# Reordering the per-unit vector work inside the matmul groups of an mLSTM and MLP kernel

## The chip, the cores and the metric

The kernel runs on one core of a Trainium2 chip. The time is that of the device in microseconds (us), the median of several runs. PE is TensorE, ACT is ScalarE, DVE is VectorE, POOL is GpSimd, and SP is SyncE, which here only issues transfers.

## The reference

Two stages follow each other. An mLSTM recurrence runs over 768 time steps for 4 batches of 8 heads with 40 features each, and a two-layer MLP is applied to its 3072 output rows of 320 features.

```
m_new  = maximum(f_gate + m, i_gate)
f_stab = exp(f_gate + m - m_new);  i_stab = exp(i_gate - m_new)
C = f_stab * C + i_stab * outer(v, k)
n = f_stab * n + i_stab * k
y = sigmoid(o_gate) * (C @ q) / maximum(abs(n . q), 1)
...
h = x @ w_in                     # 320 -> 2048
out = (h * sigmoid(h)) @ w_out   # 2048 -> 320
```

All inputs and the output are float32.

## The kernel before, in words

**Units.** The recurrence is cut into 24 units: a unit is one chunk of 64 time steps for half of the batches, 128 rows. Inside a unit the recurrence is a masked attention of the chunk with itself plus a term with the state `Cm` that earlier chunks left. Three units (384 rows) make one step of the MLP, so there are 8 steps.

**MLP.** The 2048 hidden features of a step are 16 chunks of 128. For chunk `k` the first product goes into a PSUM bank (`spot`), ACT computes a tanh (`rise`, L922), DVE the gated value `th` (L925), ACT a rounded high part `gh` (L934), DVE the remainder `gl` (L938, both of `part`), and the second product accumulates into `pout`. Both products are made from high parts and remainders, three matmuls for one, as pairs on the two halves of the array's rows. From chunk 18 on (`FIRST`) a group `k` of the last loop issues on PE the upper half of chunk `k` and the lower half of chunk `k-1`, and the second product of chunks `k-4` and `k-3`. `first_product` of group `k` lets its lower half wait for the tanh of chunk `k-2`.

**Blocks.** Into the groups of step `j` the three units of step `j+1` are woven; they are called A, B and C here. `places` gives the groups: 3, 7 and 11 in step 1, and 1, 5 and 9 from step 2 on. `at[0]` is the unit whose block stands in this group, `at[1]` the one whose block stood a group ago, and so on. A block (`block`) is, on PE between the first and second products, the scores of the next unit, the unit's own values, and the new state (`state`, L733), for which two `spot` banks are taken; the second is the one that the `th` of the same group gives back. Then follow, on DVE, the division and the output gate (`norm`, `level`, `scale`) and a 32-wise transpose into the single buffer `xt` (`turn_out`, L804), and on POOL the state's decay (`carry`: multiply L783, add L792).

**Around a block.** In the later groups a unit is transposed through memory: SP writes `xt` out (`turn_away`, L810, in `at[1]`) and reads it as `px` (`turn_in`, L818, in `at[3]`; for C in `at[1]`). `xput` then puts it in front of the next step's first product: ACT rounds `px` to `xh` (L847) and DVE takes the remainder `xl` (L848), for A and B in `at[6]`, for C in `at[4]`. So A's `xput` is in the group that is `at[2]` of B, and B's in that of C.

**Preparing the next units.** `turn` loads units ahead and makes on POOL the decay exponents `am` (`shift`, L530). In `at[2]` come `misc` of the next unit (`gate`, a tanh on ACT, L544; `look`, an exponential on ACT, L551; `near`, the scaled queries `qt` on POOL, L555) and `add` of the one after (POOL, L538); in `at[3]` the exponential of `D` (`exp`, ACT, L541) and the weighted keys (`keys`, DVE, L590).

**Weights.** The weights of the first pass through the MLP are used whole; for the others each of 8 pieces of `w_in` and `w_out` is split once into a high part (ACT: L345 for `i`, L336 for `o`) and a remainder (DVE: L347, L338) by `split_in` and `split_out`. `LOWS` names the chunk in whose tanh and `gh`/`gl` these two instructions are put.

**Order.** Each engine runs its instructions in program order, written by hand: what stands behind a waiting instruction on an engine waits too.

Of the kernel before, what the change touches and what calls it, by code (L numbers as in the profile page):

```python
# [22 lines left out]
NU = NC * NP  # L23
# [3 lines left out]
UPS = 3  # L27
# [15 lines left out]
FIRST = NFC + LAG  # L43
# [3 lines left out]
def mlstm_mlp_kernel(  # L47
# [281 lines left out]
    def split_out(i):  # L329

        if not woh:
            woh[0] = pg.tile([128, NFC, DM], F32R, tag="g", name="woh")
        full, hi = wo.pop(i), woh[0][:, 2 * i : 2 * i + 2, :]
        to, tag = (pq, "wo") if i else (pw, "wt")
        wol[i] = to.tile([128, 2, DM], F32R, tag=tag, name=f"wol{i}")
        nc.scalar.copy(hi, full)  # L336
        yield
        nc.vector.tensor_tensor(out=wol[i], in0=full, in1=hi.bitcast(F32), op=ALU.subtract)  # L338

    def split_in(i):  # L340

        whole, hi = wi.pop(i), wh[:, 0:2, i * WC : (i + 1) * WC]
        to, tag = (pi, "wi") if i else (pw, "wt")
        wl[i] = to.tile([128, 2, WC], F32R, tag=tag, name=f"wl{i}")
        nc.scalar.copy(hi, whole)  # L345
        yield
        nc.vector.tensor_tensor(  # L347
            out=wl[i], in0=whole, in1=hi.bitcast(F32), op=ALU.subtract
        )
# [652 lines left out]
    units = [Unit(n) for n in range(NU)]  # L1002
    AROUND = set(range(2 * UPS, NU)) - {3 * UPS - 1}
    free, spot = [], {}
    steps = {}
# [66 lines left out]
    for _ in range(2):  # L1072
# [115 lines left out]
    SPLITS = {"i": split_in, "o": split_out}  # L1188
# [3 lines left out]
        (0, 15): ["i2"],  # L1192
        (1, 0): ["i3"],
        (1, 1): ["o0"],
        (1, 3): ["o1"],
        (1, 4): ["i4"],
        (1, 5): ["o2", "i5"],
        (1, 7): ["o3"],
        (1, 8): ["i6"],
        (1, 9): ["o4"],  # L1200
        (1, 11): ["i7"],
        (1, 12): ["o5"],
        (1, 13): ["o6"],
        (1, 14): ["o7"],
    }
    KEYS = {5: 4, 8: 5, 12: 6, 15: 7}

    def places(k):
        j, fc = divmod(k, NFC)
        if j >= NSTEP - 1:  # L1210
            return {}
        return {fc - a: units[(j + 1) * UPS + u] for u, a in enumerate(PLACES[min(j, 2)])}

    def splits(k):
        return [SPLITS[x[0]](int(x[1])) for x in LOWS.get(divmod(k, NFC), ())]

    for k in range(FIRST):
        j, fc = divmod(k, NFC)
        st, at = steps[j], places(k)
        if j == 0 and fc in KEYS:  # L1220
            units[KEYS[fc]].keys()
        st.mm1(fc)
# [26 lines left out]
    def relay(m):  # L1249

        turn = nc.scalar.nop(nofuse=True)
        tc.add_manual_dep(turn.ins, m.ins.name, WAIT, reason="row tiles")
        return turn
# [5 lines left out]
    def first_product(k, lo, hi, turn=None):  # L1259

        both = []
        if k <= LAST:
            if lo == 0:
                spot[k] = free.pop(0)
            both.append((0, k, steps[k // NFC].rows(k % NFC, 0)))
        if k > FIRST:
            both.append((1, k - 1, steps[(k - 1) // NFC].rows((k - 1) % NFC, 1)))
        n = len(both[0][2])
        for i in range(lo, min(hi, n)):
            cols = (slice(0, NT),)  # L1270
            if i > 0 and more[0] > 0:
                more[0] -= 2 * len(both)
                cols = (slice(0, NT // 2), slice(NT // 2, NT))
            for c in cols:
                for h, g, (w, x) in [(h, g, ops[i]) for h, g, ops in both]:
                    m = nc.tensor.matmul(  # L1276
                        spot[g][:, c],
                        w,
                        x[:, c],
                        start=(h == 0 and i == 0),  # L1280
                        stop=(h == 1 and i == n - 1),
                        skip_group_check=True,
                    )
                    if h == 1:
                        follow(m, turn)
                        turn = None
        return m

    def second_product(p, k, turn=None):

        st, fc = steps[k // NFC], k % NFC
        if fc == 0 and p == 0:
            st.po = [psO.tile([128, DM], F32, tag="o", name=f"pout{st.j}_{t}") for t in range(UPS)]
        for f in (fc, fc + 1):
            gh, gl = st.g[f]
            hi, lo = woh[0][:, f, :], wol[f // 2][:, f % 2, :]
            for i, (g, w) in enumerate(((gh, hi), (gh, lo), (gl, hi))):
                for h in range(2):
                    t = (p + h) % UPS
                    m = nc.tensor.matmul(  # L1300
                        st.po[t],
                        g[half(h), t * UT : (t + 1) * UT],
                        w[half(h)],
                        start=(f == 0 and i == 0 and (p, h) in ((0, 0), (0, 1), (1, 1))),
                        stop=(f == NFC - 1 and i == 2 and (p, h) in ((1, 0), (2, 0), (2, 1))),
                        skip_group_check=True,
                    )
                    follow(m, turn)
                    turn = None
        return m  # L1310

    last_turn, rises = None, {}
    for k in range(FIRST, LAST + 2):
        at = places(k)
        even = k % 2 == 0
        old = k - 4 - k % 2
        ready = FIRST - LAG <= old and k <= LAST
        if k == FIRST:
            last_turn = relay(first_product(k, 0, 8))
        elif k == FIRST + 1:  # L1320
            first_product(k, 0, 8, last_turn)
            last_turn = None
        elif even and ready:
            first_product(k, 0, 4, rises[k - 2])
            last_turn = relay(second_product(0, old, last_turn))
            first_product(k, 4, 8)
        else:
            first_product(k, 0, 8, rises[k - 2])
        new = steps[(k - 1) // NFC]
        parts = splits(k - 1)  # L1330
        if k > FIRST:
            new.rise((k - 1) % NFC, parts)
            rises[k - 1] = new.tanh
        if 0 in at:
            block(at[0].n)
        last = steps[old // NFC] if ready and old % NFC == NFC - 2 else None
        if ready:
            m = second_product(1 if even else 2, old, last_turn)
            if 0 not in at:
                for t in ((1,) if even else (0, 2)) if last else ():  # L1340
                    last.store(t)
                last_turn = relay(m)
        if k > FIRST:
            new.part((k - 1) % NFC, parts)
        if 0 in at:
            n = at[0].n
            late = n in AROUND and n % UPS == UPS - 1
            if n + 1 < NU and not late:
                units[n + 1].weigh()
            at[0].norm()  # L1350
            at[0].hold()
            if ready:
                last_turn = relay(m)
            at[0].level()
            at[0].scale()
            at[0].carry(steps=(0,))
            at[0].carry(steps=(1,))
            if at[0].n in AROUND:
                at[0].turn_out()
            if n + 1 < NU and late:  # L1360
                units[n + 1].weigh()
        if 1 in at:
            n = at[1].n
            if n in AROUND and n % UPS == UPS - 1:
                at[1].turn_away()
                if n + 2 < NU:
                    units[n + 2].load_q()
                    units[n + 2].shift()
                at[1].turn_in()
                if n + 3 < NU:  # L1370
                    units[n + 3].load()
            else:
                turn(n)
                if n in AROUND:
                    at[1].turn_away()
        if 2 in at and at[2].n + 1 < NU:
            units[at[2].n + 1].misc()
            if at[2].n + 2 < NU:
                units[at[2].n + 2].add()
        if 3 in at and at[3].n + 2 < NU:  # L1380
            units[at[3].n + 2].exp()
            units[at[3].n + 2].keys()
        if 3 in at and at[3].n in AROUND and at[3].n % UPS < UPS - 1:
            at[3].turn_in()
        for back in (4, 6):
            if back in at and at[back].n in AROUND and (at[back].n % UPS == UPS - 1) == (back == 4):
                at[back].xput(steps[k // NFC + 1])

    st = steps[NSTEP - 1]
    st.mm2(NFC - 4)  # L1390
# [82 lines left out]
```

## Time and profile before

| | |
|---|---|
| time, median of 3 runs | 456.69 us (456.0 to 457.86) |
| time of the profiled execution | 454.56 us |
| its span, first to last instruction | 452.8 us |
| PE busy | 429.4 us (95%) |
| DVE, ACT, POOL busy | 289.3, 220.9, 152.0 us |
| mean granted TensorE clock | 0.988 of full speed |

The last loop runs from about 85 us to the end. Busy time of PE is modelled at the ends of matmuls, so a row of PE that starts after a wait tells more than the share. Where ACT begins the tanh of a group the group's first product has just ended, so that the distances between these rows are the lengths of the groups.

### The profile page before, as it was taken

How to read it: one execution, taken by the hardware profiler on the slowest of the kernel's cores; microseconds unless marked ns; L12 is line 12 of the kernel's file. 1: busy time of each engine (PE TensorE's matmuls, PEld its weight loads, DVE VectorE, ACT ScalarE, POOL GpSimd, SP SyncE). 2: the span in 40 equal slices, each digit the busy share in tenths (PEclk: the TensorE clock that was granted, in tenths of full speed). 3: DMA queues.
4: the chain of work that ended last, by engine and by line, in shares of the span. 5: the costliest groups of instructions: out<-in, count | busy, mean ns of one | idle time of the engine just before them, and what ended most of it. 6: DMA issues, size and time to landing. Idle time of an engine off the chain costs nothing.

```text
span 452.8 us, 16276 instructions
## 1 busy us (share of the span) xinstructions
PE 429.4 (95%) x6864; PEld 392.7 (87%) x6864; DVE 289.3 (64%) x588; ACT 220.9 (49%) x481; POOL 152.0 (34%) x168
## 2 busy tenths in 40 slices
PE   8999999998899989999899998999989999999996
PEld 4667677898789989899889998899988999999995
DVE  5788889378786675466764665646766566544442
ACT  7694867465464443444443532435344344434331
POOL 5835234064623634045521454215632321000000
PEclk9999999999999998999999996999999999999999
DMA  8999989165410666026560375504744041101001
GB/s 250 358 364 260 291 246 232 45 157 164 126 41 15 181 184 183 8 42 184 151 189 4 116 178 129 143 4 144 178 99 145 3 104 38 36 1 45 1 2 45
DMA packets 63401, 57.60 MB, mean 127 GB/s; under 512 B 31808, under 2 KB 49936, under 8 KB 63328
## 3 DMA queue, kind: packets, MB, share of 16 engines
q1 hardware_dynamic: 63056, 56.20, 44.2%
q8 instruction: 54, 0.88, 0.8%
q10 hardware_dynamic: 208, 0.26, 0.2%
q14 instruction: 19, 0.16, 0.1%
q0 software_dynamic: 64, 0.10, 0.1%
HBM read 49.09 MB, written 7.36 MB: 125 GB/s over the span
## 4 chain that ended last, share of the span: by engine, by line
PE 43%; issue 25%; DMA 10%; DVE 8%; ACT 7%; POOL 5%; SPq 1%; POOLq 0%; ACTq 0%; DVEq 0%
PE spot L1276 16%; PE pout L1300 14%; DVE th L925 4%; PE pout L973 4%; PE ph L891 4%; ACT D L541 2%; DMA wro<-in_w_out_dram 2%; DVE xl L848 2%; DMA vb<-in_vp_dram 2%; PE p L659 2%; DMA wri<-in_w_in_dram 2%; ACT th L922 2%; DMA D<-LFd 2%; POOL D L538 2%; PE spot L733 1%
## 5 line engine op out<-in xcount | busy, mean ns | idle before, releaser
L1276 PE MATMUL spot<-xh,wh 64*128 64x384 f32 (+1 forms) x674 | 142.4, 342 | 5.5 <-ACT th L922 4.9
L1300 PE MATMUL pout<-woh,gh 64*128 64x320 f32 x648 | 121.0, 315 | 0.0
L1300 PE MATMUL pout<-wol,gh 64*128 64x320 f32 x648 | 118.8, 308 | 0.4 <-DVE wol L338 0.4
L1300 PE MATMUL pout<-woh,gl 64*128 64x320 f32 x648 | 118.8, 308 | 0.0
L1276 PE MATMUL spot<-xl,wh 64*128 64x384 f32 (+1 forms) x569 | 117.3, 334 | 0.0
L922 ACT ACTIVATE th<-spot 128x384 f32<-128x384 f32 x110 | 53.8, 489 | 116.4 <-PE spot L1276 116.2
L938 DVE TENSOR_TENSOR gl<-th,gh 128x384 fp32r<-128x384 f32 x112 | 65.9, 589 | 57.2 <-ACT gh L934 53.1
L1276 PEld LDWEIGHTS spot<-xh,wh 64*128 64x128 f32 x674 | 92.4, 186 | 10.1 <-ACT th L922 6.8
L925 DVE SCALAR_TENSOR_TENSOR th<-th,spot 128x384 f32<-128x384 f32 x110 | 60.4, 549 | 63.2 <-ACT th L922 63.1
L934 ACT CAST gh<-th 128x384 fp32r<-128x384 f32 x112 | 57.4, 513 | 77.5 <-DVE th L925 71.5
L1276 PE MATMUL spot<-xh,wl 64*128 64x384 f32 (+1 forms) x454 | 92.7, 334 | 0.0
L1300 PEld LDWEIGHTS pout<-woh,gh 64*128 64x128 f32 x648 | 81.3, 186 | 0.9
L1300 PEld LDWEIGHTS pout<-wol,gh 64*128 64x128 f32 x648 | 81.1, 187 | 0.7 <-DVE wol L338 0.7
L1300 PEld LDWEIGHTS pout<-woh,gl 64*128 64x128 f32 x648 | 80.9, 187 | 0.0
L1276 PEld LDWEIGHTS spot<-xl,wh 64*128 64x128 f32 x569 | 73.4, 187 | 0.0
L783 POOL TENSOR_TENSOR Cm<-Cm,lq 40x328 f32<-40x328 f32 x40 | 33.3, 831 | 118.7 <-PE p L659 117.2
L1276 PEld LDWEIGHTS spot<-xh,wl 64*128 64x128 f32 x454 | 60.7, 187 | 0.0
L555 POOL TENSOR_TENSOR qt<-qk,lq 104x512 f32<-104x512 f32 x22 | 29.1, 1324 | 88.8 <-ACT lq L551 59.2
L848 DVE TENSOR_TENSOR xl<-px,xh 128x384 fp32r<-128x384 f32 x17 | 30.5, 1796 | 8.1 <-ACT xh L847 8.1
L792 POOL TENSOR_TENSOR Cm<-Cm,pk 40x328 f32<-40x328 f32 x32 | 28.4, 887 | 2.4
L973 PE MATMUL pout<-wo,g 128*128 128x320 f32 x96 | 29.0, 436 | 0.0
L538 POOL TENSOR_TENSOR D<-D,am 128x512 f32<-128x512 f32 x20 | 26.1, 1304 | 6.8 <-DVE wo L302 4.5
(161 smaller groups left out, 554.8 us busy)
## 6 DMA issues: line engine op xcount, KB each, us to landing
qk<-in_qk_dram SPq DMA_DIRECT2D x24, 512.0 KB, 6.2
ko<-in_ko_dram SPq DMA_DIRECT2D x24, 320.0 KB, 5.2
wro<-in_w_out_dram SPq DMA_DIRECT2D x8, 640.0 KB, 6.0
wri<-in_w_in_dram SPq DMA_DIRECT2D x8, 512.0 KB, 5.5
D<-LFl SPq DMA_DIRECT2D x32, 128.0 KB, 3.2
lq<-LFl SPq DMA_DIRECT2D x32, 128.0 KB, 4.0
vb<-in_vp_dram SPq DMA_DIRECT2D x48, 82.0 KB, 5.0
out_dram<-ob SPq DMA_DIRECT2D x45, 80.0 KB, 2.1
```

The source lines that it names most:

```text
L538: nc.gpsimd.tensor_tensor(out=self.Dm, in0=self.Dm, in1=self.am, op=ALU.add)
L555: nc.gpsimd.tensor_tensor(out=self.qt, in0=self.q[:KS], in1=self.lq[:KS], op=ALU.mult)
L783: nc.gpsimd.tensor_tensor(out=v, in0=v, in1=self.lq[r, :, L - 1].unsqueeze(2).broadcast_to([D, H, D1]), op=ALU.mult,)
L792: nc.gpsimd.tensor_tensor(out=v, in0=v, in1=self.both[r].rearrange("p d j f -> p (d j) f"), op=ALU.add)
L848: nc.vector.tensor_tensor(out=lo, in0=px[:, a, :], in1=hi.bitcast(F32), op=ALU.subtract)
L922: self.tanh = nc.scalar.activation(th, ph, AF.Tanh, scale=0.5)
L925: nc.vector.scalar_tensor_tensor(out=th, in0=th, scalar=1.0, in1=ph, op0=ALU.add, op1=ALU.mult)
L934: nc.scalar.copy(gh, th)
L938: nc.vector.tensor_tensor(out=gl, in0=th, in1=gh.bitcast(F32), op=ALU.subtract)
L973: nc.tensor.matmul(self.po[t], g[:, ts], w, start=(fc == 0 and i == 0), stop=(last and i == len(ops) - 1), skip_group_check=(j == NSTEP - 1),)
L1276: m = nc.tensor.matmul(spot[g][:, c], w, x[:, c], start=(h == 0 and i == 0), stop=(h == 1 and i == n - 1), skip_group_check=True,)
L1300: m = nc.tensor.matmul(st.po[t], g[half(h), t * UT : (t + 1) * UT], w[half(h)], start=(f == 0 and i == 0 and (p, h) in ((0, 0), (0, 1), (1 ...
```

## The change

`gate` of the next unit goes from `at[2]` to the block's own group, behind `hold` and its wait. `carry` does multiply and add of one half before the other half. `add` goes from `at[2]` to the end of `at[1]`, the exponential of `D` from `at[3]` to `at[2]`, and `xput` stands ahead of `look` and `near` instead of behind them and `turn_in`. The weight pieces `i4` and `o1` are split in group 18 behind its first product, `i5`, `i6` and `i7` at the end of the groups with the blocks of units 6, 7 and 8, and `o2`, `o4` and `o5` one group earlier than before.

```diff
@@ LOWS
-        (1, 3): ["o1"],
-        (1, 4): ["i4"],
-        (1, 5): ["o2", "i5"],
+        (1, 4): ["o2"],
         (1, 7): ["o3"],
-        (1, 8): ["i6"],
-        (1, 9): ["o4"],
-        (1, 11): ["i7"],
-        (1, 12): ["o5"],
+        (1, 8): ["o4"],
+        (1, 11): ["o5"],
...
+    BEHIND = {2 * UPS: ["i5"], 2 * UPS + 1: ["i6"], 2 * UPS + 2: ["i7"]}
@@ the loop over groups
-        if k > FIRST:
+        if k == FIRST:
+            for x in (split_in(4), split_out(1)):
+                next(x)
+                next(x, None)
+        else:
             new.rise((k - 1) % NFC, parts)
             rises[k - 1] = new.tanh
@@ if 0 in at
                 last_turn = relay(m)
+            if n + 1 < NU:
+                units[n + 1].gate()
             at[0].level()
             at[0].scale()
-            at[0].carry(steps=(0,))
-            at[0].carry(steps=(1,))
-            if at[0].n in AROUND:
+            at[0].carry()
+            if n in AROUND:
                 at[0].turn_out()
             if n + 1 < NU and late:
                 units[n + 1].weigh()
+            for x in BEHIND.get(n, ()):
+                for _ in SPLITS[x[0]](int(x[1])):
+                    pass
@@ behind turn, in if 1 in at
-        if 2 in at and at[2].n + 1 < NU:
-            units[at[2].n + 1].misc()
-            if at[2].n + 2 < NU:
-                units[at[2].n + 2].add()
-        if 3 in at and at[3].n + 2 < NU:
-            units[at[3].n + 2].exp()
-            units[at[3].n + 2].keys()
-        if 3 in at and at[3].n in AROUND and at[3].n % UPS < UPS - 1:
-            at[3].turn_in()
+            if n + 2 < NU:
+                units[n + 2].add()
         for back in (4, 6):
             if back in at and at[back].n in AROUND and (at[back].n % UPS == UPS - 1) == (back == 4):
                 at[back].xput(steps[k // NFC + 1])
+        if 2 in at:
+            n = at[2].n
+            if n + 1 < NU:
+                units[n + 1].look()
+                units[n + 1].near()
+            if n + 2 < NU:
+                units[n + 2].exp()
+        if 3 in at:
+            n = at[3].n
+            if n + 2 < NU:
+                units[n + 2].keys()
+            if n in AROUND and n % UPS < UPS - 1:
+                at[3].turn_in()
```

## Rows read from the trace of the kernel before

**Rows 1.** Waits of PE: line, releaser, us in total, times, longest us.

```profile
PE spot L733 <- DVE th L925: 9.9, 10, 1.6
PE spot L1276 <- ACT th L922: 4.9, 6, 1.0
```

**Rows 2.** Timeline of PE, step 3: start, duration, instruction, idle before and releaser.

```profile
221.63 0.47 PE L733 MATMUL spot<-vb,kw 64*40 64x41 f32 x26 [1.54 <-DVE th L925]
...
235.52 0.44 PE L1276 MATMUL spot<-xh,wh 64*128 64x384 f32 x1 [1.01 <-ACT th L922]
```

**Rows 3.** Timeline of ACT, step 3, groups 6 to 9 and 12 to 14.

```profile
211.36 0.49 ACT L922 ACTIVATE th<-spot 128x384 f32<-128x384 f32 x1 [3.21 <-PE spot L1276]
...
213.49 0.49 ACT L922 ACTIVATE th<-spot 128x384 f32<-128x384 f32 x1
214.60 0.51 ACT L934 CAST gh<-th 128x384 fp32r<-128x384 f32 x1 [0.62 <-DVE th L925]
215.02 0.47 ACT L544 ACTIVATE ko<-ko 128x320 f32<-128x320 f32 x1
215.39 0.62 ACT L551 ACTIVATE lq<-lq 104x512 f32<-104x512 f32 x1
215.91 0.50 ACT L847 CAST xh<-px 128x384 fp32r<-128x384 f32 x1
216.68 0.49 ACT L922 ACTIVATE th<-spot 128x384 f32<-128x384 f32 x1 [0.27 <-PE spot L1276]
...
219.97 0.62 ACT L541 ACTIVATE D<-D 128x512 f32<-128x512 f32 x1
220.50 0.47 ACT L922 ACTIVATE th<-spot 128x384 f32<-128x384 f32 x1
...
231.18 0.49 ACT L922 ACTIVATE th<-spot 128x384 f32<-128x384 f32 x1 [0.27 <-PE spot L1276]
...
235.00 0.47 ACT L922 ACTIVATE th<-spot 128x384 f32<-128x384 f32 x1
...
238.18 0.49 ACT L922 ACTIVATE th<-spot 128x384 f32<-128x384 f32 x1 [1.14 <-PE spot L1276]
```

**Rows 4.** Timeline of DVE, step 3.

```profile
213.40 0.56 DVE L938 TENSOR_TENSOR gl<-th,gh 128x384 fp32r<-128x384 f32 x1 [0.58 <-ACT gh L934]
...
216.50 2.55 DVE L848 TENSOR_TENSOR xl<-px,xh 128x384 fp32r<-128x384 f32 x1 [0.79 <-ACT xh L847]
...
225.27 0.58 DVE L804 STREAM_TRANSPOSE xt<-x 128x384 f32<-128x384 f32 x1 [0.78 <-DMA xd<-xt]
...
237.13 0.55 DVE L848 TENSOR_TENSOR xl<-px,xh 128x384 fp32r<-128x384 f32 x1
```

**Rows 5.** Timeline of POOL, step 3.

```profile
211.66 1.04 POOL L530 TENSOR_TENSOR am<-mask,aT 128x512 f32<-128x512 f32 x1
216.09 1.30 POOL L555 TENSOR_TENSOR qt<-qk,lq 104x512 f32<-104x512 f32 x1 [3.38 <-DMA D<-LFl]
217.34 1.29 POOL L538 TENSOR_TENSOR D<-D,am 128x512 f32<-128x512 f32 x1
```

**Rows 6.** Timeline of ACT, step 1: a tanh, and one weight copy.

```profile
89.03 0.49 ACT L922 ACTIVATE th<-spot 128x384 f32<-128x384 f32 x1 [2.77 <-PE spot L1276]
...
100.44 0.72 ACT L336 CAST woh<-wo 128x640 fp32r<-128x640 f32 x1
```

**Rows 7.** Timeline of SP, step 3: the two reads of A and B.

```profile
212.58 0.47 SPq L818 DMA_DIRECT2D px<-xd x1
...
225.22 0.38 SPq L818 DMA_DIRECT2D px<-xd x1
```

**Rows 8.** DMA issues of the page: count, KB each, us from issue to landing.

```profile
px<-xd SPq DMA_DIRECT2D x17, 192.0 KB, 2.5
```

**Rows 9.** Stretches behind block C, steps 2 and 4; after POOL: granted clock, DMA share, GB/s.

```profile
169.00:173.05 4.05, 4.05 (x34) 4.05 (x34) 2.29 (x6) 0.00 (x0) 3.54 (x4) 0.58 0.38 85
...
278.00:283.00 5.00, 5.00 (x44) 5.00 (x44) 1.59 (x5) 0.49 (x1) 2.71 (x3) 0.62 0.45 108
```

## The prediction, on record before the change was run

> **What bounds the kernel now.** I read the waits of PE first, then the timelines of PE, ACT, DVE and POOL over one step of the last loop, then SP and the transfers, then the granted clock. PE waits for little: ten times for the `th` that gives a block its second bank and six times for a tanh, 14.8 us in all [rows 1]. The size of these waits is better read from the tanh rows of ACT, one per group. In step 3 they lie 2.13 us apart (211.36 to 213.49) and 3.19 us apart (213.49 to 216.68), which is what PE needs for an odd and an even group; but 216.68 to 220.50 is 3.82 us where 2.13 is due, so block C's tanh is 1.69 late, and 231.18 to 235.00 is again 1.69 too long [rows 3]. PE shows these as 1.54 and 1.01 [rows 2]. Nothing of it is won back: the group behind the second takes 3.18 us (235.00 to 238.18), the usual length [rows 3]. So in this loop a tanh that comes late by some time costs that time whole.
>
> Why they are late: A's `xl` on DVE begins at 216.50 and takes 2.55 us; C's, with nothing on POOL, takes 0.55 [rows 4]. During the long one POOL runs `near` (216.09, 1.30 us) and `add` (217.34 to 218.63) [rows 5]; `xl` ends at 219.05, 0.42 behind the end of `add`. So DVE's subtraction of two SBUF tiles makes hardly any headway while POOL works, and `th`, `gh`, the exponential of `D` (219.97) and the tanh (220.50) queue up behind it without a gap [rows 3].
>
> The Trainium skill, SBUF — State Buffer, section Who interferes with whom, says that a DVE instruction with two SBUF inputs contends with a GpSimd one that reads SBUF, and that the one that starts first holds the shared ports for its whole length. The 2.55 against 0.55 agrees; by the rule the moved `add` is sure to hold up whichever such subtraction of DVE arrives during it, by the rows alone that could be nothing and the sum below some 4 us lower, 435.
>
> **The change, part by part.** *`xput` first, `add` away.* `xh` comes right behind `gh`, `xl` before `near` has started, so 2.0 us of blocking go from each of A's and B's `xl`. C's lateness of 1.69 occurs in five steps (1 to 5), the one behind B's `xput` (two groups after it, 235.00) in four (2 to 5): 5 x 1.69 + 4 x 1.69 = 15.2. The other five waits for `th`, small ones before block B and one in step 1, are what is left of 9.9 after 5 x 1.54: 2.2. The two other waits for a tanh are 4.9 - 4 x 1.01 = 0.9 [rows 1, 2]. They come from the exponential of `D` or weight copies just ahead of a tanh, both of which are moved. Together 18.3 to be had.
>
> *What it puts in the way.* The exponential now stands in the `xput` group. ACT there has from `gh` at 214.60 to the tanh at 216.68. The slots by the distances of the rows: `gh` 0.42, `look` 0.52, exponential 0.53 (219.97 to 220.50), `xh` about 0.41 (its 0.50 less the overlap that `gh` shows): 1.88, to 216.48, so 0.20 in hand [rows 3]. The `gate` (0.37 of a slot) goes to the block's group, where ACT stands idle for 3.21 before the next tanh [rows 3]: nothing; without that idle time it would cost its 0.37.
>
> `add` now runs right behind `am`, from 212.70 to 213.99 [rows 5]. `gl` begins at 213.40 there [rows 4]; by the 0.42 above it ends at 214.41, not at 213.96. `th` and `gh` behind it move by 0.45, the chain ends at 216.93, and the tanh is 0.25 late. In the groups behind A, which have no `xput` on ACT, the same delay fits. So 0.25 in each of two groups in four steps: 2.0. Lower bound nothing, if DVE gets in between `am` and `add`; upper bound 0.45 each, 3.6. I take 2.0. In `add`'s old place nothing is left that waits for it: the exponential comes a group earlier and POOL has finished by then.
>
> *`carry`.* Four instructions as before; the first add now needs `hold`'s copies sooner, but the state is read eight or more groups later: nothing, at most one wait on POOL.
>
> *Weights.* `i4` and `o1`: two copies on ACT, each no longer than `o`'s 0.72 us, in group 18, where ACT stands idle for 2.77 before the tanh at 89.03 [rows 6]; the remainders fit on DVE likewise: nothing. `i5` to `i7` come behind blocks, in ACT's idle time; on DVE they stand between `xt` and the next `th`, with `am` and `add` on POOL at their side, and `o3` to `o5` share their groups with a `gl` that `add` holds up. Bounds for the groups behind B and C of step 1: 0.25 each as in other steps, 0.5, or a whole blocked row of subtractions each, 1.69 as seen, 3.4. I take 2.0, as there are two subtractions in the row.
>
> *SP's chain.* No transfer is added and their order stays, but `xt` is one buffer, and C's transposes already wait 0.78 for B's write (225.27) [rows 4]; SP issues B's read, which needs the same landing, at 225.22 [rows 7]. With block C some 2 us earlier and SP's queue at its old pace, this wait grows by up to 1.8. Behind it stand on DVE the weighing of the next scores and `th`, for which ACT's `gh` waits. In steps 2, 4 and 5 C's transposes do not wait, so there the first 1 to 2 us are free. Bounds: nothing, or 1.8 in each of four steps, 7.2. I take 1.0, since one step of four has no reserve.
>
> *Clock.* In steps 2 and 4 the granted clock falls to its lower level of 1.2 GHz for part of the time behind C's wait: 0.58 over 4.05 us and 0.62 over 5 us, that is 1.7 + 1.9 = 3.6 us of full-speed work lost [rows 9]. Behind blocks A and B, with at most short waits, there is no such stretch. I take these as gone with the wait; bounds 0 and 3.6.
>
> *Sum.* 18.3 - 2.0 - 2.0 - 1.0 = 13.3. The profiled execution took 454.56 us (span 452.8): 441.3, and 437.7 without the clock losses. The median of the runs, 456.69, lies 2.1 above the profiled one; I carry half of that over, since some of it may be the same clock: 439.
>
> **The rivals.** A difference of 0.5% (2.3 us) is about what can be told from none here.
>
> *POOL gets the ports first all the same.* `xl` would start at about 216.06 and `near` at 216.58, by the distances of their rows [rows 3 to 5]. If POOL won, `xl` would end 0.42 behind `near`, near 218.3 instead of 216.6. The next group has lost its exponential, so some 0.6 stay per `xput`, nine times: about 444. For it: the lead is only half a microsecond. Against: `xl` runs already. The rule of the Trainium skill named above (SBUF — State Buffer) would also let `xl` through. Chance 0.10.
>
> *The transfers bind at C.* The full 7.2 instead of 1.0: 445. For it: the 0.78 that is there already. Against: three of four steps have reserve. Chance 0.11.
>
> *The clock losses stay*, as the block itself has small matmuls: 439 + 3.6, 443. Chance 0.07.
>
> *ACT is held up by `px`: slower.* `xput` now stands ahead of `look`, the exponential and the next tanh, so that a transfer that lands late stops them all, at the full price shown above. A's `px` is issued at 212.58 [rows 7] and lands 2.5 later [rows 8], at 215.1; the new `xh` asks for it at about 215.5 (gh at 215.05 plus 0.42). B's lands at 227.7 and is asked for at about 227.9. The margins are 0.4 and 0.2. Nine groups do this; from 2.0 us of lateness beyond the margin in each, 18 us, the gain of 17.7 is used up, and at 2.5 us the time is 461. Before, `gate` and `look` covered 0.9 of it. Against: the issue follows `at[1]` of the same step, and the longest landing is not far from 2.5. Chance 0.07, and 0.05 that it and the transfers at C together bring the time back to within 0.5%.
>
> **The chances and the range.** The forecast has 0.60, the three smaller gains 0.28: faster 0.88, same 0.05, slower 0.07. The predicted time is 439. Low: nothing of the new losses and the clock back, 454.56 - 18.3 - 3.6 = 432.7, so 432. High: 445 of the transfers plus the clock's 3.6, 449. The forecast's own range is 434 to 443.
>
> **What would show it.** `xl` of A and B at about 0.55 us, not 2.55, in all steps. No wait of 1.5 for `th` before block C's state, no wait of 1.0 behind B's `xput`; tanh rows at 2.13 and 3.19 there. `gl` of the group behind a block lengthened, to about 1.0, with `add` beside it. The two stretches of lower clock gone. The prediction is wrong if ACT's `xh` shows idle time for a transfer of `px`, if `xt` waits 2 us or more for `xd` in every step, if `near` begins before `xl` and `xl` stays at 1.8 or more, or if the tanh of `xput` groups comes more than 0.5 late.

## The result and the profile after

The changed kernel takes 436.91 us (median of 4 runs, 436.32 to 439.45), the kernel before in the same series 456.35 us (4 runs, 455.84 to 457.86). The ratio is 0.958, 95% interval 0.9535 to 0.9624. The profiled execution took 436.81 us with a span of 435.0, that is 17.8 less than the span before; its mean granted clock is 0.998 of full speed instead of 0.988.

The first view is that of PE's waits: line, releaser, total, times, longest.

```profile
PE spot L1273 <- ACT th L922: 1.9, 3, 0.8
...
PE spot L733 <- issue: 0.2, 1, 0.2
```

Line 733 no longer waits for `th` (ten times, 9.9 us in [rows 1]), and the waits of the first product for a tanh went from 4.9 to 1.9. (Line 1273 of the changed kernel is line 1276 of before.) Next the timeline of ACT in step 3, against [rows 3].

```profile
202.47 0.47 ACT L544 ACTIVATE ko<-ko 128x320 f32<-128x320 f32 x1 [0.81 <-PE pout L1297]
204.76 0.49 ACT L922 ACTIVATE th<-spot 128x384 f32<-128x384 f32 x1 [1.81 <-PE spot L1273]
...
206.88 0.49 ACT L922 ACTIVATE th<-spot 128x384 f32<-128x384 f32 x1 [0.45 <-PE spot L1273]
208.62 0.51 ACT L934 CAST gh<-th 128x384 fp32r<-128x384 f32 x1 [1.24 <-DVE th L925]
209.04 0.51 ACT L847 CAST xh<-px 128x384 fp32r<-128x384 f32 x1
209.45 0.63 ACT L551 ACTIVATE lq<-lq 104x512 f32<-104x512 f32 x1
209.99 0.62 ACT L541 ACTIVATE D<-D 128x512 f32<-128x512 f32 x1
210.51 0.47 ACT L922 ACTIVATE th<-spot 128x384 f32<-128x384 f32 x1
...
212.62 0.49 ACT L922 ACTIVATE th<-spot 128x384 f32<-128x384 f32 x1 [0.51 <-PE spot L1273]
...
220.08 0.49 ACT L922 ACTIVATE th<-spot 128x384 f32<-128x384 f32 x1 [0.37 <-PE spot L1273]
...
223.74 0.47 ACT L922 ACTIVATE th<-spot 128x384 f32<-128x384 f32 x1
...
225.86 0.49 ACT L922 ACTIVATE th<-spot 128x384 f32<-128x384 f32 x1 [0.52 <-PE spot L1273]
```

C's tanh now comes 2.11 us behind the one before it (210.51 to 212.62), where before it was 3.82 [rows 3]; likewise 223.74 to 225.86 behind B's `xput`. What is new are 3.63 us (206.88 to 210.51) and 3.66 (220.08 to 223.74) where 3.19 is due: from `gh` at 208.62 to the tanh, ACT runs without a gap. The timelines of DVE (with a row of step 2 at the start and one of step 4 at the end) and of POOL tell why.

```profile
168.51 0.58 DVE L804 STREAM_TRANSPOSE xt<-x 128x384 f32<-128x384 f32 x1 [1.58 <-DMA xd<-xt]
...
206.46 1.66 DVE L938 TENSOR_TENSOR gl<-th,gh 128x384 fp32r<-128x384 f32 x1 [0.58 <-ACT gh L934]
208.04 0.54 DVE L925 SCALAR_TENSOR_TENSOR th<-th,spot 128x384 f32<-128x384 f32 x1
...
209.64 0.55 DVE L848 TENSOR_TENSOR xl<-px,xh 128x384 fp32r<-128x384 f32 x1
...
217.55 0.58 DVE L804 STREAM_TRANSPOSE xt<-x 128x384 f32<-128x384 f32 x1 [0.70 <-DMA xd<-xt]
...
256.46 0.58 DVE L804 STREAM_TRANSPOSE xt<-x 128x384 f32<-128x384 f32 x1 [2.16 <-DMA xd<-xt]
```

```profile
205.29 1.04 POOL L530 TENSOR_TENSOR am<-mask,aT 128x512 f32<-128x512 f32 x1
206.41 1.30 POOL L538 TENSOR_TENSOR D<-D,am 128x512 f32<-128x512 f32 x1
210.16 1.29 POOL L555 TENSOR_TENSOR qt<-qk,lq 104x512 f32<-104x512 f32 x1 [2.46 <-DMA D<-LFl]
```

`xl` takes 0.55 and is nearly done when `near` begins. `add` starts 0.05 ahead of `gl`, which ends at 208.12, 0.41 behind `add`'s end, and `th` comes late by it. Last, the stretches around block C in steps 2 and 4 (columns as in [rows 9]). Before, the lower clock stood ahead of the tanh that ends the block's group, at 173.05 and 282.25; that tanh is now at 168.04 and 268.60, and the granted clock ahead of it is full.

```profile
163.00:168.00 5.00, 5.00 (x156) 4.95 (x150) 2.92 (x10) 1.57 (x5) 3.16 (x4) 1.00 0.61 152
...
262.00:267.00 5.00, 5.00 (x165) 4.70 (x163) 3.42 (x10) 2.38 (x6) 1.75 (x2) 1.00 0.84 220
267.00:272.00 5.00, 5.00 (x66) 5.00 (x64) 3.70 (x8) 1.50 (x3) 4.26 (x5) 1.00 0.39 81
```

### The profile page after: what moved, and what is told of

It reads as the page before. It is cut to its first block, busy times and chain, and to the rows that moved or that the text cites. A ratio compares the mean times of both kernels' runs of the same rounds, so it can differ in the third digit from the quotient of the medians.

```text
span 435.0 us, 16240 instructions
## 1 busy us (share of the span) xinstructions
PE 424.5 (98%) x6864; PEld 388.2 (89%) x6864; DVE 280.2 (64%) x588; ACT 222.7 (51%) x481; POOL 156.6 (36%) x168
## 4 chain that ended last, share of the span: by engine, by line
PE 59%; issue 19%; DMA 9%; DVE 5%; ACT 4%; SPq 3%; POOL 0%; POOLq 0%; DVEq 0%; ACTq 0%
PE spot L1273 20%; PE pout L1297 16%; PE ph L891 7%; PE pout L973 6%; DMA xd<-xt 5%; PE p L571 2%; PE p L659 2%; PE p L642 2%; SPq L810 1%; DVE th L925 1%; DMA qk<-in_qk_dram 1%; DMA vb<-in_vp_dram 1%; DVE gl L938 1%; PE spot L733 1%; ACT gh L934 1%
## 5 line engine op out<-in xcount | busy, mean ns | idle before, releaser
L1273 PE MATMUL spot<-xh,wh 64*128 64x384 f32 (+1 forms) x674 | 146.1, 339 | 2.7 <-ACT th L922 1.9
L1273 PE MATMUL spot<-xl,wh 64*128 64x384 f32 (+1 forms) x569 | 119.4, 333 | 0.0
L938 DVE TENSOR_TENSOR gl<-th,gh 128x384 fp32r<-128x384 f32 x112 | 77.4, 691 | 62.1 <-ACT gh L934 51.4
L1273 PEld LDWEIGHTS spot<-xh,wh 64*128 64x128 f32 x674 | 95.0, 184 | 7.9 <-ACT th L922 5.0
L1273 PE MATMUL spot<-xh,wl 64*128 64x384 f32 (+1 forms) x454 | 94.5, 330 | 0.0
L783 POOL TENSOR_TENSOR Cm<-Cm,lq 40x328 f32<-40x328 f32 x40 | 34.2, 855 | 115.3 <-PE p L659 113.7
L1273 PEld LDWEIGHTS spot<-xl,wh 64*128 64x128 f32 x569 | 74.5, 185 | 0.0
L1273 PEld LDWEIGHTS spot<-xh,wl 64*128 64x128 f32 x454 | 62.5, 185 | 0.0
L792 POOL TENSOR_TENSOR Cm<-Cm,pk 40x328 f32<-40x328 f32 x32 | 29.9, 936 | 2.5
```

The lines of the kernel that those rows point to most:

```text
L783: nc.gpsimd.tensor_tensor(out=v, in0=v, in1=self.lq[r, :, L - 1].unsqueeze(2).broadcast_to([D, H, D1]), op=ALU.mult,)
L792: nc.gpsimd.tensor_tensor(out=v, in0=v, in1=self.both[r].rearrange("p d j f -> p (d j) f"), op=ALU.add)
L938: nc.vector.tensor_tensor(out=gl, in0=th, in1=gh.bitcast(F32), op=ALU.subtract)
L1273: m = nc.tensor.matmul(spot[g][:, c], w, x[:, c], start=(h == 0 and i == 0), stop=(h == 1 and i == n - 1), skip_group_check=True,)
```

## The experiments

One yardstick serves for all. The lateness of a tanh row is its distance from the one before it, less what the steady rows take (2.13 or 3.19, 5.33 with a block). Summed over the last loop it is 25.1 us before and 7.0 after; the difference, 18.1, is the 17.8 of the spans and 0.3 by which the last loop begins later (first tanh at 89.33 instead of 89.03). The table has the median time, that sum of the profiled execution, and the lateness in step 3 of four rows: the one before C's tanh, C's own, and the same pair three and four groups behind C's. A dash is under 0.13.

| kernel | median us | sum | before C's | C's | 3 behind | 4 behind |
|---|---|---|---|---|---|---|
| before | 456.35 | 25.1 | – | 1.69 | – | 1.69 |
| `xput` ahead alone | 443.44 | 14.4 | – | 0.80 | – | 0.82 |
| `add` early alone | 442.48 | 14.4 | – | 0.51 | – | 0.80 |
| these two together | 436.15 | 6.4 | 0.26 | – | 0.30 | – |
| after | 436.91 | 7.0 | 0.44 | – | 0.47 | – |
| after, `xput` behind | 436.50 | 6.2 | – | – | 0.22 | – |
| after, `add` and exponential back | 438.28 | 8.7 | – | 0.53 | – | 0.45 |
| after, `gate` and `carry` back | 440.19 | 10.0 | 0.24 | – | 0.58 | – |
| after, weights back | 436.72 | 7.1 | 0.24 | – | – | – |
| after, `am` a block earlier | 435.05 | 5.0 | – | – | – | – |
| after, two buffers for `xt` | 438.85 | 10.6 | 0.25 | – | 0.22 | – |
| both of the last two | 435.60 | 7.2 | 0.63 | – | – | – |
| `am` earlier, `xput` behind | 434.62 | 5.5 | 0.29 | – | – | – |

Each new kernel has four runs, beside runs of the kernel before whose medians lay between 455.69 and 455.90.

**`xput` ahead alone**, on the kernel before:

```diff
+        for back in (4, 6):
+            if back in at and at[back].n in AROUND and ...:
+                at[back].xput(steps[k // NFC + 1])
         if 2 in at and at[2].n + 1 < NU:
             units[at[2].n + 1].misc()
...
-        for back in (4, 6):
...
```

> The kernel before with one edit: xput stands ahead of gate, look, near and add; everything else in its old place. Theory (DVE's xl is blocked by POOL's near and add): xl of A and B falls from 2.55 to about 0.55 us, but add still runs behind near and the exponential of D still waits for it just ahead of the next tanh, so about 0.8 of the 1.69 stays at block C and behind B's xput; gain 0.85 x 9 = 7.6 and perhaps some clock: about 447 us (445 to 450). Rival (what counts is the exponential of D ahead of the tanh on ACT, the length of xl is hidden): within 2 us of before, 455 to 458.

443.44 us (442.53 to 444.35), ratio 0.974 (0.969 to 0.979): a larger gain than expected, 12.5. By the tanh rows the nine late ones (C's in steps 1 to 5, the one behind B's `xput` in steps 2 to 5) give 7.5 of it (15.2 of lateness before, 7.7 here), as expected; the two stretches of lower clock, which are gone as well, give 4.5. `xl` is at 0.55 everywhere, yet C's tanh stays 0.80 late. The timeline of ACT shows what holds it, and the group of the exponential its sum.

```profile
214.21 0.63 ACT L541 ACTIVATE D<-D 128x512 f32<-128x512 f32 x1 [0.76 <-POOL D L538]
214.75 0.47 ACT L922 ACTIVATE th<-spot 128x384 f32<-128x384 f32 x1
```

```profile
L541 ACT ACTIVATE D<-D 128x512 f32<-128x512 f32 x20 | 12.6, 631 | 11.3 <-POOL D L538 11.3
```

So there was a second cause under the first: the exponential waits for `add` itself, 11.3 us over the loop, and the tanh stands behind it on ACT. In the kernel before, the longer delay by `xl` covered it. There it was also shorter, by an estimate from its rows: `add` ended at 218.63 [rows 5], and with the exponential's 0.53 behind it [rows 3] C's tanh would have been 0.35 late. The rest of the 0.80 is about the 0.41 by which `xh`, now ahead of `look` on ACT, delays `near` and `add`.

**`add` early alone**, on the kernel before:

```diff
                 turn(n)
                 if n in AROUND:
                     at[1].turn_away()
+            if n + 2 < NU:
+                units[n + 2].add()
         if 2 in at and at[2].n + 1 < NU:
             units[at[2].n + 1].misc()
-            if at[2].n + 2 < NU:
-                units[at[2].n + 2].add()
```

> The kernel before with one edit: add goes from at[2] to the end of at[1]; the exponential and xput stay. Theory (blocked by POOL): xl now waits for near alone and takes about 1.3 us; lateness at C and behind B's xput about 0.55 in place of 1.69, and gl of the group behind each block is held up to about 1.6 us by add; about 447 to 449 us. Rival (only the order of xput and near matters): xl stays above 2 us and the time within 2 us of before.

442.48 us (439.74 to 444.49), ratio 0.972 (0.966 to 0.977), again a larger gain than expected, with the stretches of lower clock gone here too. Here the first cause is left, at less than half its size, as the timelines of DVE and of ACT show:

```profile
215.61 1.30 DVE L848 TENSOR_TENSOR xl<-px,xh 128x384 fp32r<-128x384 f32 x1 [0.80 <-ACT xh L847]
216.84 0.54 DVE L925 SCALAR_TENSOR_TENSOR th<-th,spot 128x384 f32<-128x384 f32 x1
```

```profile
217.41 0.51 ACT L934 CAST gh<-th 128x384 fp32r<-128x384 f32 x1 [1.20 <-DVE th L925]
217.83 0.62 ACT L541 ACTIVATE D<-D 128x512 f32<-128x512 f32 x1
218.36 0.47 ACT L922 ACTIVATE th<-spot 128x384 f32<-128x384 f32 x1
```

`xl` is held by `near` alone, 1.30 instead of 2.55, and `th`, `gh`, the exponential and the tanh follow it without a gap. The profiled execution is the slowest of the four: 3.7 us of its sum come from a standstill of PE in step 2 and the lower clock behind it, which the last section takes up.

**Both together**, on the kernel before, with `gate`, the exponential, `carry` and the weights in their old places (the two diffs above).

> The kernel before with xput in front of misc and with add behind turn, both at once; gate, the exponential of D, carry and the weights stay as before. Alone the two gave 443.44 and 442.48, 12.5 and 13.4 us less than before. Theory that they are two ways round the same collision: nearly nothing is added, and what is left is the crowding of ACT by gate, exponential and tanh; so 441 (439.5 to 442.5). Rival, that each takes away losses of its own: with both the time comes to that of the whole change, 436 to 438, and the moves of gate and exponential are worth nothing.

436.15 us (435.94 to 436.45), ratio 0.956 (0.951 to 0.960): the rival was right, and this is the whole gain. Alone the two gave 12.5 and 13.4 against their own runs of before, together 19.5. They are neither one collision met twice nor a plain sum. The 4.5 us of lower clock go with either edit and count once. And a tanh is as late as the later of two paths: `xput` ahead clears the path over `xl`, `add` early clears the path over the exponential and shortens that over `xl`. Of the 15.2 us of the nine late rows 7.7 are left with the one edit, 6.0 with the other and nothing with both. ACT, with the exponential left in its old group (last three rows: `gh`, exponential, tanh), is on time:

```profile
210.14 0.47 ACT L922 ACTIVATE th<-spot 128x384 f32<-128x384 f32 x1
211.23 0.52 ACT L934 CAST gh<-th 128x384 fp32r<-128x384 f32 x1 [0.62 <-DVE th L925]
211.65 0.62 ACT L541 ACTIVATE D<-D 128x512 f32<-128x512 f32 x1
212.27 0.49 ACT L922 ACTIVATE th<-spot 128x384 f32<-128x384 f32 x1
```

210.14 to 212.27 is 2.13, the steady length. The crowding of ACT that was expected to cost did not in this group.

**After, `xput` put back behind** `keys` and `turn_in` (the loop over `back` moved to the end of the vector work).

> The changed kernel with one edit undone: xput stands behind look, near, the exponential and keys again. Theory: near starts before xl, which then takes about 0.8 us, as most of near is over; th of the group is 0.45 late, which costs about 0.4 at block C in five steps and nothing behind B's xput: about 439 us (438 to 441). Rival (xput ahead of near is what brings the gain): most of the 1.69 comes back nine times, 448 to 452 us.

436.50 us (435.56 to 437.48), ratio 0.959 (0.955 to 0.963): as after, and below both ranges that had been given. `xl` does meet `near` again, but not `add`:

```profile
210.15 0.78 DVE L848 TENSOR_TENSOR xl<-px,xh 128x384 fp32r<-128x384 f32 x1 [0.95 <-ACT xh L847]
```

and in the next group ACT no longer has an exponential between `gh` and the tanh, since it went a group up. So with `add` early, the early `xput` and the early exponential stand in for each other: the kernel with both parts has only the first, this one only the second, and that with `add` early alone, which has neither, is late by 0.51 and 0.80. (The last also has `gate` ahead of `look`, so that `near` starts later there.)

**After, `add` back** in `at[2]` behind `near`, the exponential back in `at[3]`:

```diff
-            if n + 2 < NU:
-                units[n + 2].add()
...
                 units[n + 1].near()
             if n + 2 < NU:
-                units[n + 2].exp()
+                units[n + 2].add()
         if 3 in at:
             n = at[3].n
             if n + 2 < NU:
+                units[n + 2].exp()
                 units[n + 2].keys()
```

> The changed kernel with add back in at[2] behind near and the exponential of D back in at[3]. Theory: the exponential waits for add again, 0.4 late at C (five times) and behind B's xput (four times), 0.37 before block B (four times), against 0.45 won where gl is no longer held up behind a block: 437 to 440 us. Rival (that the moved add and exponential carry the gain): 445 us or more.

438.28 us (436.45 to 440.56), ratio 0.963 (0.958 to 0.968), as expected; the runs overlap with those of after. The exponential waits for POOL again:

```profile
212.63 0.63 ACT L541 ACTIVATE D<-D 128x512 f32<-128x512 f32 x1 [0.49 <-POOL D L538]
```

Beside `xput` ahead alone this wait is 0.49 instead of 0.76. The edits that differ between the two kernels are `gate`, `carry` and the weights; `gate` is 0.37 of ACT ahead of `look`, and `near` waits for `look`. So with `add` in its old place these other moves are worth 5.2 us (443.44 against 438.28), although with `add` early they are worth nothing that can be measured.

**After, `gate` back** in `at[2]` ahead of `look`, and `carry` in two rounds.

> The changed kernel with gate back in at[2] ahead of look, and carry in two rounds again. Theory: the group with xput, look and the exponential has no room on ACT, so gate's 0.37 is paid nine times there and about 0.2 five times in the groups behind A: about 441 us (439.5 to 442); carry costs nothing. Rival (ACT has room, gate is hidden wherever it stands): 436 to 438 us.

440.19 us (439.15 to 440.92), ratio 0.966 (0.962 to 0.970), as expected; `carry` was not undone by itself. With the exponential moved up, `gate` has no room in that group:

```profile
223.48 0.51 ACT L934 CAST gh<-th 128x384 fp32r<-128x384 f32 x1 [1.03 <-DVE th L925]
...
224.31 0.47 ACT L544 ACTIVATE ko<-ko 128x320 f32<-128x320 f32 x1
...
225.73 0.47 ACT L922 ACTIVATE th<-spot 128x384 f32<-128x384 f32 x1
```

From `gh` to tanh it is 2.25, 0.58 late. Once `add` is early, `gate`'s move pays only for the exponential's: with neither, the kernel of both parts above is as fast as after.

**After, weights back** (`LOWS` as before, no `BEHIND`, nothing in group 18).

> The changed kernel with the weight pieces split in their old groups (LOWS as before, nothing behind blocks or in group 18). Theory: only step 1 changes; o2 and i5 together make th before the second block about 0.9 late, and i6 in a group with xput and the exponential makes a tanh 0.5 late; about 439 us (438 to 440.5). Rival (the weight pieces carry a large part of the gain, as step 1 lost more than 5 us before): 441 us or more.

436.72 us (436.23 to 440.41), ratio 0.960 (0.955 to 0.966): no difference, where a loss of about 2 had been expected and one of 4 or more was the rival. Step 1 loses as much, only in other groups.

**After, `am` a block earlier**: `add` finds its exponents made, and `shift` runs behind it for the unit after (its call in `turn` is left out, except for unit 6).

```diff
...
             if n + 2 < NU:
                 units[n + 2].add()
+            if n + 3 < NU:
+                units[n + 3].shift()
```

> The changed kernel with one more edit: am of a unit is made a block earlier, behind add, so that add runs straight behind carry and is over when gl arrives. Theory (POOL's add holds up gl behind blocks, and the tanh of the next group with it): gl there falls from 1.65 to 0.6 or 0.7 us, the 0.45 goes in about seven groups and most of 1.2 + 0.6 in step 1: 432 to 434 us. Rival (those tanh are late because ACT's queue of xh, look and the exponential is full): 436 to 438 us.

435.05 us (433.03 to 437.56), ratio 0.956 (0.950 to 0.963). The median lies between the two ranges; the profiled execution, 433.42, lies in that of the theory. Its trace has the mechanism: `gl` behind blocks B and C of step 3 takes 1.19 and 1.07, not 1.66 and 1.61, as POOL is further on when it arrives (0.6 to 0.7 had been expected):

```profile
204.96 1.19 DVE L938 TENSOR_TENSOR gl<-th,gh 128x384 fp32r<-128x384 f32 x1 [0.58 <-ACT gh L934]
...
217.96 1.07 DVE L938 TENSOR_TENSOR gl<-th,gh 128x384 fp32r<-128x384 f32 x1 [0.58 <-ACT gh L934]
```

Lateness in step 3 is gone, and the sum falls by 2.1; the intervals of this kernel and of after overlap all the same.

**After, two buffers for `xt`** (taken from a pool of two instead of one).

> The changed kernel with two buffers for xt. Theory (the single buffer waits for the write of the unit before): the waits of xt for a transfer, 9.1 us in eight, are gone; of that only what reached a tanh counts, 1.1 in step 4 and twice 0.4 in step 2: 435 us (434 to 436). Rival (the waits are wholly hidden): 436.5 to 437.5 us.

438.85 us (435.04 to 441.14), ratio 0.962 (0.956 to 0.969): a miss. The four executions lie apart: 435.04 and 437.33 with a mean granted clock of 1.00, 440.37 (the profiled one) and 441.14 with 0.992. The 9.1 us of waits of `xt` are gone, with them the lateness of 1.12 in step 4 behind the wait of 2.16 above. But a group later in that step 1.48 us are lost to another transfer, by the timeline of ACT:

```profile
263.87 0.51 ACT L847 CAST xh<-px 128x384 fp32r<-128x384 f32 x1 [1.17 <-DMA px<-xd]
...
265.34 0.47 ACT L922 ACTIVATE th<-spot 128x384 f32<-128x384 f32 x1
```

This is the rival that the prediction held for slower, `xh` waiting for `px` with everything behind it, though in one group only. And PE stands still in block B of step 2; its timeline, and stretches of 2 us there (columns as in [rows 9]):

```profile
153.01 0.22 PE L733 MATMUL spot<-vb,kw 64*40 64x41 f32 x1 [2.00 <-issue]
```

```profile
150.00:152.00 2.00, 1.01 (x72) 0.90 (x65) 1.02 (x2) 0.71 (x2) 0.00 (x0) 1.00 1.00 280
...
154.00:156.00 2.00, 2.00 (x16) 2.00 (x16) 1.83 (x6) 0.28 (x1) 1.85 (x3) 0.50 0.25 62
```

"Issue" is time in which the engine waited for nothing that the profile shows. With the lower clock behind it, this costs 5.0 us of lateness in one group. That the second buffer brings it about is not shown: `add` early alone has it with one buffer, and single executions of after (439.45, clock 0.994) and of the kernel with the weights back (440.41, 0.992) show a clock like it.

**Both of the last two.**

> The kernel after with both of the last two edits: the decay exponents made one block earlier, and two buffers for the transposed values. Theory that the lateness of tanh rows is what is left to be had: the decay exponents alone gave 435.05, and the two buffers took away the waits of the transposes, of which 1.0 us or so came late at a tanh; so 434 (432.5 to 435.5). Rival: earlier writes by the second buffer fill the DMA engines in step 2 while block B stands on PE, so that PE stands still for about 2 us at line 733 with no releaser and the granted clock falls behind it, as in the run with two buffers alone; then 436 to 439 again, with such a row in the trace between 150 and 160 us.

435.60 us (433.84 to 435.84), ratio 0.953 (0.949 to 0.958). Both of these losses are there again, 3.2 us of lateness in step 2 and 0.83 in step 4, by the timelines of PE and of ACT; `xh` also waits 0.73 for `px` in step 3, where the tanh is 0.63 late:

```profile
151.20 0.22 PE L733 MATMUL spot<-vb,kw 64*40 64x41 f32 x1 [1.57 <-issue]
```

```profile
259.91 0.51 ACT L847 CAST xh<-px 128x384 fp32r<-128x384 f32 x1 [0.93 <-DMA px<-xd]
```

So in both profiled executions what two buffers save is given back. The rival's row is there, the rival's time is not: 435.60 lies just above the theory's range.

**`am` a block earlier and `xput` behind.**

> The kernel after with the decay exponents made one block earlier and xput put back behind keys and turn_in. Theory that with add gone from its old place the order of xput is worth nothing: 435 (433.5 to 436.5), as with the decay exponents alone. Rival, that the place of xput counts once gl is no longer held up, since xl then meets near again: 1 us per step more, 439 to 441, with A's and B's xl at 1.3 us or more.

434.62 us (434.38 to 435.69), ratio 0.953 (0.947 to 0.958): the order of `xput` is worth nothing here either. It is the lowest median of all; its interval overlaps that of after, so that it beats the kernel before for certain; whether it beats the changed one four runs can't tell.

## Why the prediction was right, and where not

439 was forecast, 436.91 measured. The profiled execution was to take 437.7; it took 436.81. That comes from terms of about the right size, not from large errors that cancel. Where the prediction was off is in their accounts.

*18.3 to be had.* The sum was right and the account of it incomplete. The 1.69 was put down to `xl` alone; in truth two paths led to each late tanh, `xl` (1.69) and `add` with the exponential behind it (0.35 by the rows of before, 0.80 once `xput` is ahead). So neither edit alone clears the nine rows. It made no difference to the forecast, since the change moves both.

*The order of `xput`* was credited with the 2.0 of blocking. It is right for the kernel before, wrong for the changed one: with `add` and the exponential gone from there, `xput` behind `near` costs nothing that can be measured. The price of the rival that POOL gets the ports first, 0.6 for each `xput`, was too high for the same reason: with `xput` behind, no tanh that follows such an `xl` in step 3 is more than 0.24 late. Whether POOL could win with `xput` ahead did not come up: `xl` began 0.52 before `near`.

*`add` beside `gl`*: 0.25 in each of eight groups was forecast, 2.0 in all; the eight tanh are 2.4 late, unevenly, from 0.02 to 0.47. In step 3 it is 0.44 and 0.47, at the upper bound of 0.45. The part that was mis-sized there is the distance: `add` was put 0.70 ahead of `gl`, and it starts 0.05 ahead, so it holds `gl` nearly for its whole length. Counted from block B's tanh, `gl` comes 0.34 earlier (1.70 behind it instead of 2.04, with 0.51 of waiting for the write of `xt` instead of 1.07), and `add` 0.31 later than forecast (1.65 instead of 1.34). With the weights back, where steps 2 to 5 run the same program, the eight are 0.9 late, so the size also changes from one execution to the next. The next step of the working held: `gl` ends 0.41 behind `add`, forecast 0.42. The Trainium skill, SBUF — State Buffer, section Who interferes with whom, has the one that issues first hold the shared ports for its whole length and the other blocked; 1.66 against 0.56 agrees.

*`gate`* in the block's group costs nothing, as forecast: 1.81 of idle time stands behind it. *The exponential* has the room that was worked out: `gh` to tanh takes 1.89 us (208.62 to 210.51), forecast 1.88.

*Step 1* (the prediction's weights): 2.0 forecast; two losses of 1.23 and 1.21 stand there (0.63 of the second stood there before), and the other four of before, 4.1 in all, are gone. The first is seen in the timelines of DVE and of POOL:

```profile
109.22 1.20 DVE L338 TENSOR_TENSOR wol<-wo,woh 128x640 fp32r<-128x640 f32 x1
110.34 1.65 DVE L938 TENSOR_TENSOR gl<-th,gh 128x384 fp32r<-128x384 f32 x1
```

```profile
108.36 1.37 POOL L530 TENSOR_TENSOR am<-mask,aT 128x512 f32<-128x512 f32 x1
109.81 1.76 POOL L538 TENSOR_TENSOR D<-D,am 128x512 f32<-128x512 f32 x1
```

With `add` back in its old place both groups take the due 3.20. With the weights in their old places they are still 0.60 and 1.17 late, and another group is 0.73. So this is a price of `add`; the weights' move only shifts where it is paid and is worth nothing either way. Both losses are in groups with an `xput`: the prediction had named a tanh more than 0.5 late there as a sign that it is wrong, and in step 1 that sign came, though from the rows of `add` and not from `xput`.

*SP's chain*: 1.0 forecast. The waits of `xt` grew from 4.9 to 9.1 us, but only two reached a tanh: that of 2.16 in step 4, with 1.12 where it had been 0.57, and that of 1.58 before block C of step 2, whose next tanh is 0.42 late, 170.59 instead of 170.17 (2.13 behind 168.04):

```profile
170.59 0.48 ACT L922 ACTIVATE th<-spot 128x384 f32<-128x384 f32 x1
```

Together that is 1.0, as forecast, but the place was luck: step 3, which was held to have no reserve, waits 0.51 and 0.70, less than before, and step 2 was held to have some.

*Clock*: both stretches gone, as forecast with 3.6; by the tanh rows that ended the groups there before they had cost 1.54 and 2.95, so 4.5. They also stay away with a lateness of 0.8 and 1.1 at C (`xput` ahead alone, granted 1.00 in both places). What made the clock fall in these two steps and not behind the equal waits of steps 1, 3 and 5 is not shown.

*The rivals*: in the changed kernel ACT's `xh` waits for no `px` and the transfers do not bind at C; that they are not far from it is seen in the kernels with two buffers. *The last 1.1*, half of the distance between the profiled run and the median of before, was not needed: the median of after lies 0.1 above its profiled run.

## What to carry to other kernels

A late instruction can have two causes of different length, of which the profile names only the one that ended last; before an edit is priced, follow the second path too, here from POOL's `add` over the exponential to the tanh. When a POOL instruction of two SBUF operands is moved, look up which two-operand subtractions of DVE will arrive during it, and by how little. Undoing a set of moves one by one is not enough, since moves can stand in for each other: `xput` undone here costs nothing, `add` with the exponential 1.4 us, yet each put in alone gains more than 12. Only the two together on the old kernel showed that they give all that can be measured of the six.

## What the runs showed of the hardware

**Who gets the ports, by hundredths.** In the kernel with both parts `gl` starts 0.01 us before `add`, by the timelines of DVE and of POOL, and here it is POOL that is late:

```profile
193.34 0.56 DVE L938 TENSOR_TENSOR gl<-th,gh 128x384 fp32r<-128x384 f32 x1 [0.59 <-ACT gh L934]
```

```profile
193.35 1.71 POOL L538 TENSOR_TENSOR D<-D,am 128x512 f32<-128x512 f32 x1
```

1.71 is 0.42 more than the 1.29 of an undisturbed one; this kernel and that with `gate` and `carry` back have six such rows, 1.70 to 1.72, with DVE ahead by 0.00 to 0.02. A held-up DVE instruction likewise ends behind POOL's: in the 13 traces 162 rows of `gl` and `xl` were held by `near` or `add`, and all end 0.40 to 0.43 behind the last of them. In step 1 above, `wol` waits for `am` (to 109.73) and ends 0.69 behind it, though `add` starts at 109.81: it gets in between. In the kernel before, `xl` did not get in between `near`, which runs to 217.39, and `add`, which starts at 217.34 [rows 5]. The 0.08 is seen again at `carry`, five times in after: `gl` starts at 138.37, 0.01 behind a multiply that ends at 139.10, the addition behind it starts at 139.18 and takes 1.09 instead of 0.89, and `gl` ends at 139.52, 0.42 behind the multiply. So in these traces DVE gets in where POOL leaves 0.08 us between two instructions, and not where the rows of two join.

**A standstill of PE without a releaser.** 2.00 and 1.57 us in the kernels with two buffers, 1.89 in that with `add` early alone, which has one buffer; 0.20 to 0.79 at the same place in seven others, none in three. In the 2 us ahead of it, and at the same place in the three without it, the DMA engines are busy for 0.90 to 1.05 of the time, so full DMA engines alone do not decide it. Behind the three long ones the granted clock falls to 0.50, that is 1.2 GHz, for some 3 us in two and some 7 in that with two buffers alone; behind the seven short ones it stays at 1.00.

What PE lacks is not named by a releaser, but the DMA queue that the page lists as "instruction" (54 packets, 0.88 MB) fits. One packet of 16 KB of it falls in here, in the kernel with two buffers from 150.47 to 151.73. Between 150.4 and 151.8 the queue's row is this; between 148 and 150.4 it has none.

```profile
q8 instruction: 1, 0.02, 5.6%
```

In all ten kernels PE resumes 1.19 to 1.46 us behind the end of this packet, so the later it ends the longer PE stands. In the three long cases it starts 0.90 to 1.26 us behind the first matmul of the block's scores, in the other ten kernels between 0.49 ahead of that matmul and 0.06 behind it. So PE seems to wait for its own next instructions. No run moved that queue, and why the packet comes late in these three stays open.
